# Input tiles with a 64-value slot for each head's 48 values

## The chip, the cores and the metric

The kernel runs on one core of a Trainium2 chip. Its time is the device time of one execution in microseconds (us). Several runs are given by their median. A profile is one execution recorded by the hardware profiler; its span runs from the first to the last recorded instruction.

## What is computed

Two parts follow each other. A gated recurrence runs over 4 batches, 8 heads, 768 steps and a head size of 48, and its output feeds a feed-forward part with the largest of three products in place of an activation.

```python
# q, k, v, alpha: (4, 8, 768, 48) float32
for t in range(S):
    state = alpha[:, :, t, :, None] * state + einsum('bhd,bhe->bhde', k[:, :, t], v[:, :, t])
    y[:, :, t] = einsum('bhd,bhde->bhe', q[:, :, t], state)
# y, heads side by side, becomes x: (3072, 384)
h = maximum(maximum(x @ w1, x @ w2), x @ w3)   # w1, w2, w3: (384, 768)
out = h @ w_out                                # w_out: (768, 384); out: (3072, 384) float32
```

## The kernel before

The recurrence is cut into six blocks of 128 time steps. One step of the kernel takes one block of two batches (16 pairs of batch and head, `NH`), so that there are 12 steps. Time steps stand on the 128 partitions.

For each step, `load` (L81 to L87) fetches four tiles, `ra`, `rk`, `rq` and `rv`, from `alpha`, `k`, `q` and `v`, in this order, by one DMA each on the queue of SyncE (SP, L85). In memory an input is ordered batch, head, time, value; a tile has the time on the partition and 16 x 48 values in it. So one DMA moves 128 x 16 rows of 48 values, which are 192 bytes each, and 384 KB in all. Every one of the four names has four buffers (`raw`, `bufs=4`).

The pieces that read these tiles are few. `logs` (L137) is one ScalarE instruction that takes the logarithm of `ra` into `la`, whose rows are 64 values apart. `decays` multiplies the logarithms by a triangular matrix on TensorE, takes two exponentials on ScalarE, and multiplies `rk` and `rq` by them into `qk` (L159 and L160); this is done on VectorE in steps 0 to 2 and on GpSimd later. `values` (L170) scales `rv` into float16 on ScalarE.

The other pieces work on what these leave. `turn` transposes `qk`, `scores` and `attend` form the outputs of the recurrence, `turn_back` transposes them for the feed-forward part, `gates` (L233 and L235, GpSimd) and `update` (L254, VectorE) carry the state to the next block, `gate` (L268 to L278) forms the three products and their maximum, and `project` (L285 to L290) forms the result and stores it.

The order on every engine is written out by hand in five strings, `PROLOGUE`, `FIRST`, `SECOND`, `STEADY` and `LAST`. A letter is a piece, the digit is a part of it, and `@` gives the step. In the order of SP's queue, the loads of steps 0, 1 and 2 come first (12 DMAs), then 12 DMAs with the weights (L120 and L125), then the loads of steps 3 and 4. From then on `load(s + 3)` stands ahead of each step's pieces, and the stores of the results lie between the loads. GpSimd casts the weights to float16 in groups of three (`cast_weights`, L130, the pieces `W0` to `W3`). In GpSimd's order `W0` stands directly ahead of the gate product of step 0 (`M0@0`).

The tiles are laid out in each partition one after another: first the constant tiles and the weights, then the 16 input tiles of `raw`, then the working tiles.

Of the kernel before, what the change touches and what calls it, by code (L numbers as in the profile page):

```python
# [9 lines left out]
FP32 = mybir.dt.float32  # L10
# [13 lines left out]
def kernel(  # L24
# [14 lines left out]
    B, H, S, D = q.shape  # L39
    NT, DM = out.shape  # L40
    DF = moe_w_out.shape[0]
    P = 128
# [4 lines left out]
    NH = U * H  # L47
# [20 lines left out]
    raw = ctx.enter_context(tc.tile_pool(name="raw", bufs=4))  # L68
# [9 lines left out]
    def where(s):  # L78
        return s // (B // U), (s % (B // U)) * U

    def load(s):  # L81
        cb, b0 = where(s)
        for n in ("a", "k", "q", "v"):
            t = raw.tile([P, NH, D], FP32, name=f"r{n}", tag=f"r{n}")
            nc.sync.dma_start(  # L85
                t, ins[n][cb * P:(cb + 1) * P, b0:b0 + U].rearrange("s b h d -> s (b h) d"))
            raws[s, n] = t  # L87

    c16 = cpool.tile([P, 3 * P + 2], FP16, name="c16")
    c32 = cpool.tile([P, 6], FP32, name="c32")  # L90
    load(0)
    nc.scalar.dma_start(c16, nc.inline_tensor(c16_np, name="c16").ap())
    nc.scalar.dma_start(c32, nc.inline_tensor(c32_np, name="c32").ap())
# [240 lines left out]
    LAST = """G0 G1 G2 G3 G4 G5 G6 G7 O1 G8 O0"""  # L334

    load(1)
    load(2)
    load_weights()
    load(3)
# [43 lines left out]
```

## Time and profile before

| | |
|---|---|
| time, median of two runs | 171.71 us (170.89 and 172.54) |
| span of the profiled execution | 168.8 us |
| TensorE busy | 156.9 us, 93% of the span |
| VectorE busy | 112.2 us, 66% |
| ScalarE busy | 99.0 us, 59% |
| GpSimd busy | 49.0 us, 29% |
| DMA | 107,251 packets, 28.68 MB, of them 99,808 packets under 512 bytes |
| one input load | 384 KB, median from issue to landing 4.7 us (`ra`) to 5.8 us (`rq`) |

For the profiled execution the profile gives the span alone, so its own time outside the span is not known; the median of the two runs lies 2.9 us above the span.

How to read the profile: PE is TensorE's matrix multiplication, PEld its loading of weights, DVE VectorE, ACT ScalarE, POOL GpSimd, SP SyncE. A letter q behind a name is that engine's queue of instructions that issue DMAs or wait. L85 is line 85 of the kernel. In the rows of the slices, the span is cut into 40 equal parts and each digit is the busy share in tenths; PEclk is the clock granted to TensorE in tenths of full speed. The row DMA is the mean share of 16 DMA engines, GB/s what they moved. In a list of waits the columns are who waited, for whom, the sum in us, the number of waits, and the longest. In an order of time they are the start, the duration, the engine, the line, the operation, and in brackets the idle time before it with what ended it. The chain is the work that ended last, followed back step by step to what released it.

### The profile page before, as it was taken

The numbers are of one execution on the slowest core, as the hardware profiler recorded it, in microseconds if no ns is written. First come the engines' busy times: TensorE is split into PE (matmuls) and PEld (weight loads), VectorE is DVE, ScalarE is ACT, GpSimd is POOL, SyncE is SP. The second block draws the span as 40 slices with busy tenths as digits, with TensorE's granted clock in tenths as the row PEclk, the third lists the DMA queues.
The fourth block names the chain that finished last, engine by engine and source line by source line (L and its number), as shares of the span: only waits on it lengthen the run. The fifth ranks groups of instructions, "written<-read, shape, count | busy, mean of one in ns | idle before, by whom it ended". The sixth has DMA issues, their size and how long they took to land.

```text
span 168.8 us, 4329 instructions
## 1 busy us (share of the span) xinstructions
PE 156.9 (93%) x1758; PEld 121.1 (72%) x1758; DVE 112.2 (66%) x185; ACT 99.0 (59%) x181; POOL 49.0 (29%) x72
## 2 busy tenths in 40 slices
PE   7955859999999999999999999999999999999992
PEld 2423637699887676886877978968968869869860
DVE  4186777756647757597587587687667775975730
ACT  3616585142777684874974964956856748435232
POOL 0000005756063454404512531541442244100000
PEclk9995675599999999999999999999999999999999
DMA  6999999998999999999897967948931011020013
GB/s 131 223 219 218 176 247 336 355 360 170 226 172 213 218 248 254 192 226 221 219 223 189 235 105 177 228 91 192 212 92 50 0 56 41 0 93 4 0 47 140
DMA packets 107251, 28.68 MB, mean 170 GB/s; under 512 B 99808, under 2 KB 107232, under 8 KB 107232
## 3 DMA queue, kind: packets, MB, share of 16 engines
q1 hardware_dynamic: 106944, 28.32, 77.3%
q8 instruction: 13, 0.21, 0.6%
q10 hardware_dynamic: 288, 0.10, 0.3%
q14 instruction: 6, 0.05, 0.1%
HBM read 23.69 MB, written 4.72 MB: 168 GB/s over the span
## 4 chain that ended last, share of the span: by engine, by line
PE 81%; SPq 7%; DMA 3%; ACT 3%; DVE 2%; issue 1%; ACTq 0%
PE ops L285 14%; SPq L85 7%; PE tps L179 6%; DMA ra<-in_alpha_dram 3%; PE yps L210 3%; PE xtp L222 2%; PE lps L146 2%; PE yps L207 2%; PE sps L250 2%; PE sps L247 2%; DVE lat L196 1%; PE lps L149 1%; ACT xb L214 1%; PE gps_514 L268 1%; PE gps_523 L268 1%
## 5 line engine op out<-in xcount | busy, mean ns | idle before, releaser
L268 PEld LDWEIGHTS <-wcat 128*128 128x128 f16 x648 | 60.3, 98 | 9.0 <-POOL gm L235 0.2
L285 PE MATMUL ops<-wo_97,hT 128*128 128x384 f16 x144 | 27.1, 327 | 0.0
L288 ACT COPY ob<-ops 128x384 f32<-128x384 f32 x24 | 11.5, 480 | 14.2 <-PE ops L285 14.2
L155 ACT ACTIVATE ic<-lps,c_69 128x384 f32<-128x384 f32 x24 | 13.9, 581 | 8.4 <-PE lps L146 5.1
L285 PEld LDWEIGHTS <-hT 128*128 128x128 f16 x144 | 12.8, 98 | 7.5
L183 DVE COPY qkT<-tps 128x1024 f16<-128x1024 f16 x24 | 16.4, 683 | 1.3 <-PE tps L179 1.1
L214 ACT ACTIVATE xb<-yps,c_69 128x384 f16<-128x384 f32 x24 | 14.0, 585 | 4.8 <-PE yps L210 4.8
L156 ACT ACTIVATE ac<-lps,c_69 128x384 f32<-128x384 f32 x24 | 13.8, 575 | 0.0
L210 PE MATMUL yps<-vt,lat 128*128 128x48 f16 x192 | 12.2, 190 | 0.6 <-ACT vt L170 0.6
L193 PEld LDWEIGHTS <-qkT 48*128 48x128 f16 x192 | 6.3, 98 | 8.8 <-issue 7.7
L159 POOL TENSOR_TENSOR qk_87<-rk,ic 128x384 f16<-128x384 f32 x6 | 6.0, 997 | 21.9 <-ACT ic L155 21.9
L210 PEld LDWEIGHTS <-lat 128*128 128x128 f16 x192 | 10.5, 101 | 1.5 <-DVE lat L196 0.7
L170 ACT ACTIVATE vt<-rv,c_69 128x768 f16<-128x768 f32 x12 | 11.3, 940 | 0.0
L225 ACT COPY xT<-xtp 128x768 f16<-128x768 f16 x12 | 9.6, 803 | 1.0 <-PE xtp L222 1.0
L296 PE MATMUL wps<-blank 128*128 128x512 f16 x22 | 8.0, 528 | 1.2 <-DVE blank L343 1.2
L159 POOL TENSOR_TENSOR qk_86<-rk,ic 128x384 f16<-128x384 f32 x4 | 4.0, 997 | 15.4 <-ACT ic L155 15.4
L130 POOL CAST wcat<-ws_0_114 128x768 f16<-128x768 f32 x1 | 0.8, 823 | 26.3 <-DMA ws_0_114<-in_moe_w_dram 26.3
L159 POOL TENSOR_TENSOR qk_85<-rk,ic 128x384 f16<-128x384 f32 x4 | 4.0, 995 | 13.9 <-ACT ic L155 13.9
L207 PEld LDWEIGHTS <-qkT 128*128 128x128 f16 x80 | 7.7, 98 | 0.4
L222 PE MATMUL xtp<-c_68,xb 128*128 128x128 f16 x72 | 7.4, 228 | 0.5 <-ACT xb L214 0.3
L159 POOL TENSOR_TENSOR qk_84<-rk,ic 128x384 f16<-128x384 f32 x4 | 4.0, 996 | 12.4 <-ACT ic L155 12.4
L222 PEld LDWEIGHTS <-xb 128*128 128x128 f16 x72 | 5.2, 101 | 2.3 <-ACT xb L214 0.9
(409 smaller groups left out, 359.6 us busy)
## 6 DMA issues: line engine op xcount, KB each, us to landing
ra<-in_alpha_dram SPq DMA_DIRECT2D x12, 384.0 KB, 4.7
rk<-in_k_dram SPq DMA_DIRECT2D x12, 384.0 KB, 5.6
rq<-in_q_dram SPq DMA_DIRECT2D x12, 384.0 KB, 5.8
rv<-in_v_dram SPq DMA_DIRECT2D x12, 384.0 KB, 5.7
out_dram<-ob SPq DMA_DIRECT2D x24, 192.0 KB, 2.0
ws_0_114<-in_moe_w_dram SPq DMA_DIRECT2D x1, 384.0 KB, 4.9
ws_1_116<-in_moe_w_dram SPq DMA_DIRECT2D x1, 384.0 KB, 4.5
ws_2_118<-in_moe_w_dram SPq DMA_DIRECT2D x1, 384.0 KB, 5.0
```

Of the source, the lines that this page charges most:

```text
L85: nc.sync.dma_start(t, ins[n][cb * P:(cb + 1) * P, b0:b0 + U].rearrange("s b h d -> s (b h) d"))
L155: nc.scalar.activation(out=ic, in_=lv, func=AFT.Exp, bias=nat_c, scale=-1.0)
L156: nc.scalar.activation(out=ac, in_=lv, func=AFT.Exp, bias=at_c)
L159: eng.tensor_mul(kv, raws[s, "k"][:, hs], ic)
L170: nc.scalar.mul(vt, raws.pop((s, "v")), vs_c)
L183: nc.vector.tensor_copy(out=qkT, in_=tps)
L210: nc.tensor.matmul(yps[:, p, i, :], lat[:, i, p, :], vt[:, u * H + 2 * p + i, :], start=(cb == 0), stop=(cb == 0 or i == 1))
L214: nc.scalar.mul(xb, yps.rearrange("p a b d -> p (a b d)"), ys_c)
L222: nc.tensor.transpose(xtp[:, u, f, :], xb[:, f * P:(f + 1) * P], ident)
L268: nc.tensor.matmul(gps[:, j, :], wcat[:, f, g, jj * P:(jj + 1) * P], xT[:, f].rearrange("p u t -> p (u t)"), start=(f == 0), stop=(f == NF ...
L285: nc.tensor.matmul(ops, hT_of[s][:, jj, u * P:(u + 1) * P], wo16[:, jj, :], start=(jj == 0), stop=(jj == NJ - 1))
L288: nc.scalar.copy(out=ob, in_=ops)
```

## The change

An input tile is declared with 64 places for each pair of batch and head, and the kernel uses the first 48 of each. The values that are loaded, their order and all instructions stay the same; the rows that a load writes are 256 bytes apart instead of 192, and a tile takes 4,096 bytes of each partition instead of 3,072.

```diff
     def load(s):
         cb, b0 = where(s)
         for n in ("a", "k", "q", "v"):
-            t = raw.tile([P, NH, D], FP32, name=f"r{n}", tag=f"r{n}")
+            t = raw.tile([P, NH, 64], FP32, name=f"r{n}", tag=f"r{n}")[:, :, :D]
             nc.sync.dma_start(
                 t, ins[n][cb * P:(cb + 1) * P, b0:b0 + U].rearrange("s b h d -> s (b h) d"))
             raws[s, n] = t
```

## The prediction

> **What bounds the kernel now.** I read the page first (span, slices, chain), then the waits, then the DMA view of the first 15 us, then the order of time of SP's queue and of 26 to 31 us.
>
> ```profile
> span 168.8 us, 4329 instructions
> PE   7955859999999999999999999999999999999992
> DMA  6999999998999999999897967948931011020013
> PEclk9995675599999999999999999999999999999999
> PE 81%; SPq 7%; DMA 3%; ACT 3%; DVE 2%; issue 1%; ACTq 0%
> ```
>
> A slice is 4.2 us. From slice 8 (about 30 us) TensorE is full to the end, so there only TensorE work sets the time. The first seven slices have holes while the DMA row is at 9: this is where loads can decide. The chain agrees: 81% TensorE, and 10% the queue that issues loads and one load.
>
> ```profile
> ACT la_81 L137 <- DMA ra<-in_alpha_dram: 3.5, 1, 3.5
> ACT la_80 L137 <- DMA ra<-in_alpha_dram: 3.5, 2, 3.2
> ACT la_82 L137 <- DMA ra<-in_alpha_dram: 1.7, 1, 1.7
> POOL wcat L130 <- DMA ws_0_114<-in_moe_w_dram: 26.3, 1, 26.3
> ```
>
> All 8.7 us that compute waits for input loads are four waits of ScalarE for an alpha tile, three of them in the first 20 us; GpSimd cannot start casting weights before 26.7 us, when the first weight tile has come through behind twelve input loads.
>
> ```profile
> GB/s 0 0 0 0 6 129 244 277 263 258 236 239 246 230 222 203 224 227 223 211 206 215 232 223 216 218 214 221 219 215 204 228 225 217 212 213 219 224 217 220
> ...
> q1 hardware_dynamic: 14799, 2.82, 112.9%
> ```
>
> This is the DMA view of 0 to 15 us, 0.375 us a slice. With one load under way it moves 244 to 277 GB/s, with a backlog about 220. A load is 2048 rows of 192 bytes, 128 on each of 16 DMA engines; 192 x 16 / 220 = 14.0 ns a row and engine, and 128 x 14.0 = 1.79 us a load. SP's queue has the same step:
>
> ```profile
> 6.45 1.75 SPq L85 DMA_DIRECT2D ra<-in_alpha_dram  x1
> 8.24 1.75 SPq L85 DMA_DIRECT2D rk<-in_k_dram  x1
> 10.04 1.75 SPq L85 DMA_DIRECT2D rq<-in_q_dram  x1
> 11.83 1.75 SPq L85 DMA_DIRECT2D rv<-in_v_dram  x1
> ```
>
> Behind the twelve loads, the start of the feed-forward part hangs on these:
>
> ```profile
> 28.89 0.83 POOL L130 CAST wcat<-ws_2_118 128x768 f16<-128x768 f32 x1 [0.27 <-DMA ws_2_118<-in_moe_w_dram]
> 30.04 0.21 POOL L235 TENSOR_TENSOR gm<-gt,c_69 128x16 f32<-128x16 f32 x1
> 30.28 0.56 DVE L254 TENSOR_TENSOR st_1_89<-sps,gm 128x384 f16<-128x384 f32 x1 [0.34 <-POOL gm L235]
> ```
>
> The third weight tile releases a cast, the cast (same engine) the gate product gm, and gm the state on VectorE, which waited only 0.34 us. So a later load stream passes on nearly one for one, while an earlier one gains only until the other chain (alpha of step 2, landing at 19.4 us, then la_82) is last.
>
> [...] the products at L159 already write strided rows of 48, at 556 ns for 384 values.
>
> **The change, part by part.** The order of instructions on every engine, and SP's waits, stay as they were; only addresses and strides change.
>
> *Where rows come to lie.* The title of the change promises 256-byte boundaries. It gives the pitch, 256 bytes, but not the base. In the built program the first input tile begins 104,384 bytes into each partition, and that is 407 x 256 + 192. Tiles are 3,072 bytes before and 4,096 after, both multiples of 256, so all sixteen begin at 192 beyond a boundary. Before, rows lie at 192, 128, 64, 0 and so on: the first two of four cross a boundary. After, every row lies at 192 and crosses one. So the change doesn't do what it says; if the write side cares for boundaries at all, it is worse off.
>
> *Loads, 48 of 2048 rows.* Bytes, rows and queue order are the same, so HBM's side is. Does the write side set the 14.0 ns? The same tiles, with the same mixture of offsets, were written at 277 GB/s at the start (192 x 16 / 277 = 11.1 ns). So writes in this layout can go at 11.1 ns or better, and what holds a backlog at 14.0 is something else. [...] Lower bound: the opening rate held throughout, 11.1, which is -2.9. I take 0, since the trace has the write side faster than the pace. Each ns costs 12 x 128 x 1 ns = 1.54 us at the first weight tile.
>
> *Engine reads.* 12 logs (L137, 842 ns), 12 value scalings (L170, 948 ns) and 48 products (L159 and L160: 12 on VectorE at 556 ns, 36 on GpSimd at 996 ns) now read rows of 48 with a gap. The logs and products already write such rows. Taken at 0; a bound of +5% would be 24 x 0.045 = 1.1 us on ScalarE, busy 59%, and 36 x 0.05 = 1.8 us on GpSimd, busy 29%, both beside a TensorE that is busy 12.00 of 12 us in the windows from 72 to 120 us. In the prologue, where this cover is missing, it would be three logs, three scalings and 12 products: 3 x 0.042 + 3 x 0.047 + 12 x 0.028 = 0.6 us. For a gain nothing speaks but symmetry; I bound it by the same 0.6.
>
> *Room.* 16 tiles x 1,024 bytes = 16 KB a partition more; the tiles behind move by 16,384 bytes, a multiple of 256, so no other tile changes its offset. 0.
>
> *After the prologue.* A steady step is 11.9 us (from projection at 75.49 us to 87.42), its four loads 4 x 1.79 = 7.2 us: hidden[...].
>
> *The sum.* Span 168.8 + 0 = 168.8. What lies around the span is 171.71 - 168.8 = 2.9 us if the profiled execution was like the median. Predicted 171.7 us.
>
> **Rivals.**
>
> *Slower: each crossing costs on the write side, on top of the 14.0 ns.* Place: L85's twelve loads ahead of the weights. [...] all of it reaches the end, because TensorE is full from there[...]. It decides from 2.2 ns a row (3.4 us, 2%). For it: all rows cross instead of half, the backlog is in this stage, and the step is at SP's heels. Against: 244 to 277 GB/s at the start with half the rows crossing. [...]
>
> *Faster: writes with gaps go quicker for a reason that no view shows* (or the base is aligned after all). At 11.1 ns the ninth load, the alpha of step 2, comes 9 x 128 x 2.9 ns = 3.3 us earlier. la_82 waits 1.7 us itself and its predecessors waited 3.5, so it follows: at best -3.3, 168.4 us, just under 2%; to pass it the pace would have to go below 11.1. For it: these loads are on the chain. Against: the base at 192, the unchanged source side, and that before has the wider mixture including aligned rows.
>
> *Engine reads slow down with the gaps*, the 0.6 us above: 172.3, no change.
>
> **How the numbers follow.** No change 0.60, slower 0.30, faster 0.10. The slower case has much weight because a penalty for crossing can only go one way with this base, and because a load stream that grows later reaches the end undiminished. 2% (3.4 us) is about what a measurement of this kernel can tell from no change; its two runs alone lie 1.65 us apart. The range reaches from the faster case (168.4, rounded into 168.8) to a little over the slower one, 177.5; the likeliest case's own is 170.5 to 173.0.
>
> **What would show it right or wrong.** Right: the load step on SP's queue stays at 1.79 us, the backlog at about 220 GB/s, the first cast at 26.7 us, the first gate at 30.5 us, and L137, L170, L159 keep 842, 948 and 556/996 ns. [...] The faster one shows as a step near 1.5 us, and shorter waits of la_81 and la_82. Durations at L137 or L159 that grow by more than 5% would show the engine reads wrong. A change of the steady step from 11.9 us would make the whole argument wrong, since no part of the change reaches it here.

## The result and the profile after

The changed kernel takes 177.88 us (median of 177.53 and 178.22) against 171.71 us, slower by a ratio of 1.039 (95% interval 1.027 to 1.051). The forecast was no change. The profiled execution took 177.53 us, of which the span is 175.6 us; before it was 168.8 us. For the experiments below, the time is the median of all executions, and the ratio leaves out those in a slower state and compares the rest with the kernel before as measured beside them (medians of all 171.00 us for the first four experiments, 170.77 us for the other four).

The page's span, slices and chain after the change:

```profile
span 175.6 us, 4329 instructions
PE   7844366899999999999999999999999999999992
DMA  7999999999999999999999999999999901010013
PEclk9995576558999999999999999999999999999999
PE 79%; SPq 9%; DMA 4%; ACT 3%; DVE 2%; issue 1%; ACTq 0%
```

The work is the same, and TensorE's busy time nearly so (158.2 us, before 156.9). A slice is now 4.4 us, and TensorE is full from the ninth slice on, at about 35 us instead of 30 us: the holes at the start became longer and the rest kept its length. The two waits for loads ahead of it grew:

```profile
ACT la L137 <- DMA ra<-in_alpha_dram: 17.5, 4, 6.2
POOL wcat L130 <- DMA ws<-in_moe_w_dram: 35.1, 7, 33.1
```

ScalarE's waits for alpha tiles doubled from 8.7 to 17.5 us, and the first weight tile holds GpSimd until 33.6 us instead of 26.7 us. The DMA view of 0 to 15 us, in slices of 0.375 us, shows why:

```profile
GB/s 0 0 0 0 31 200 227 250 249 195 149 159 163 163 163 163 162 163 163 163 164 164 163 163 164 163 163 164 164 162 162 163 164 164 163 163 162 163 165 163
...
q1 hardware_dynamic: 11327, 2.16, 124.0%
```

In the opening the loads run at up to 250 GB/s (before, up to 277). Then, in the backlog, where loads are issued faster than they finish, they sit at 163 GB/s, almost without scatter, where before they had about 220. That is 192 x 16 / 163 = 18.8 ns a row and engine instead of 14.0. SP's queue shows the same step, from start to start:

```profile
7.76 2.35 SPq L85 DMA_DIRECT2D ra<-in_alpha_dram  x1
10.15 2.35 SPq L85 DMA_DIRECT2D rk<-in_k_dram  x1
12.55 2.36 SPq L85 DMA_DIRECT2D rq<-in_q_dram  x1
14.95 2.35 SPq L85 DMA_DIRECT2D rv<-in_v_dram  x1
```

2.40 us a load instead of 1.79. Over twelve loads this is 12 x 0.61 = 7.3 us at the first weight tile. In the order of time on GpSimd and on VectorE:

```profile
33.58 0.82 POOL L130 CAST wcat<-ws 128x768 f16<-128x768 f32 x1 [33.14 <-DMA ws<-in_moe_w_dram]
...
36.04 0.83 POOL L130 CAST wcat<-ws 128x768 f16<-128x768 f32 x1 [0.57 <-DMA ws<-in_moe_w_dram]
...
37.20 0.21 POOL L235 TENSOR_TENSOR gm<-gt,c 128x16 f32<-128x16 f32 x1
...
37.44 1.02 DVE L254 TENSOR_TENSOR st<-sps,gm 128x384 f16<-128x384 f32 x2 [1.42 <-POOL gm L235]
```

The first cast starts 6.85 us later (26.73 before), the gate product 7.16 us (30.04), the state 7.16 us (30.28), and the span is 6.8 us longer. But these pieces are not what the end waited for. The chain runs over another load, the alpha of step 2, the ninth. First before, then after:

```profile
13.63 5.76 DMA ra<-in_alpha_dram
...
30.58 1.39 PE gps_514 L268 x6
```

```profile
17.34 7.67 DMA ra<-in_alpha_dram
...
36.66 2.67 PE gps L268 x12
```

That load lands 5.6 us later (25.0 us for 19.4), and the first gate on TensorE starts 6.1 us later (36.59 us for 30.51), 2.2 us after its weights have been cast. The 36 gate matmuls that follow the next outputs of the recurrence take 4.5 us (39.80 to 44.31) instead of 3.9 (33.72 to 37.66), at a lower granted clock: it was 0.75 from 40 to 42 us, and before 1.00 from 34 to 36 us. These two make 6.7 of the 6.8 us. All other steps stand still: L137 has a median of 844 ns, L170 948 ns, L159 556 ns on VectorE and 1,002 ns on GpSimd, and a steady step takes 11.94 us (projection at 82.23 and 94.17 us in the chain).

### The profile page after: what moved, and what is told of

It reads as the page before. It is cut to its first block, busy times and chain, and to the rows that moved or that the text cites. A ratio compares the mean times of both kernels' runs of the same rounds, so it can differ in the third digit from the quotient of the medians.

```text
span 175.6 us, 4329 instructions
## 1 busy us (share of the span) xinstructions
PE 158.2 (90%) x1758; PEld 121.9 (69%) x1758; DVE 112.3 (64%) x185; ACT 99.1 (56%) x181; POOL 49.3 (28%) x72
## 4 chain that ended last, share of the span: by engine, by line
PE 79%; SPq 9%; DMA 4%; ACT 3%; DVE 2%; issue 1%; ACTq 0%
PE gps L268 42%; PE ops L285 14%; SPq L85 9%; PE tps L179 6%; PE aps L193 5%; DMA ra<-in_alpha_dram 4%; PE xtp L222 3%; PE yps L210 2%; PE lps L146 2%; PE yps L207 2%; PE sps L250 2%; PE sps L247 1%; DVE lat L196 1%; PE lps L149 1%; ACT ic L155 1%
## 5 line engine op out<-in xcount | busy, mean ns | idle before, releaser
L268 PE MATMUL gps<-xT,wcat 128*128 128x256 f16 x648 | 83.4, 276 | 0.0
L278 DVE TENSOR_TENSOR h<-gps,h 128x512 f16<-128x512 f32 x36 | 24.9, 692 | 22.0 <-PE gps L268 18.5
L276 ACT CAST h<-gps 128x512 f16<-128x512 f32 x36 | 21.1, 587 | 29.2 <-PE gps L268 28.8
L196 DVE TENSOR_TENSOR lat<-aps,c 128x512 f16<-128x512 f32 x48 | 30.8, 684 | 10.2 <-PE aps L193 10.2
L159 POOL TENSOR_TENSOR qk<-rk,ic 128x384 f16<-128x384 f32 x18 | 18.0, 1002 | 61.0 <-ACT ic L155 58.0
L278 DVE TENSOR_TENSOR hT<-gps,h 128x512 f16<-128x512 f32 x36 | 24.9, 692 | 11.1 <-PE gps L268 9.4
L285 PE MATMUL ops<-wo,hT 128*128 128x384 f16 x144 | 27.1, 327 | 0.0
L179 PE MATMUL tps<-c,qk 128*128 128x128 f16 x192 | 15.9, 231 | 6.4 <-DVE qk L160 6.0
L137 ACT ACTIVATE la<-ra 128x768 f16<-128x768 f32 x12 | 10.1, 845 | 17.5 <-DMA ra<-in_alpha_dram 17.5
L288 ACT COPY ob<-ops 128x384 f32<-128x384 f32 x24 | 11.5, 482 | 13.4 <-PE ops L285 13.4
L160 POOL TENSOR_TENSOR qk<-rq,ac 128x384 f16<-128x384 f32 x18 | 18.0, 1000 | 2.4 <-DMA rq<-in_q_dram 2.4
L214 ACT ACTIVATE xb<-yps,c 128x384 f16<-128x384 f32 x24 | 14.1, 586 | 4.9 <-PE yps L210 4.9
```

Of the source, the lines that this page charges most:

```text
L159: eng.tensor_mul(kv, raws[s, "k"][:, hs], ic)
L160: eng.tensor_mul(qv, raws[s, "q"][:, hs], ac)
L179: nc.tensor.transpose(tps[:, i, p, :], qk[:, i, u * HP + p].rearrange("p a b -> p (a b)"), ident)
L196: nc.vector.tensor_mul(lat[:, i], aps[i], mask.unsqueeze(1).broadcast_to([P, HP, P]))
L268: nc.tensor.matmul(gps[:, j, :], wcat[:, f, g, jj * P:(jj + 1) * P], xT[:, f].rearrange("p u t -> p (u t)"), start=(f == 0), stop=(f == NF ...
L276: nc.scalar.copy(out=h, in_=gps)
```

## The experiments

The offset of a row is how far behind a 256-byte boundary of its partition it begins. Three theories were set against each other. A: a row that a load writes is paid by the 256-byte blocks that it touches, so one that crosses a boundary costs twice. B: the price of a row grows with its offset. C: the gap between rows costs, wherever they begin. Before, the pace of 14.0 ns fits A (one and a half blocks of 9.4 ns, half of the 18.8 after) and B (offsets of 96 bytes on average, where after they are 192) alike. A straight line through these two paces, as an estimate, gives B 12.4 ns at offset 64 and 15.6 ns at 128; what tells them apart is the offset.

### Rows at offset 0

The edit is against the changed kernel.

```diff
+    lead = ctx.enter_context(tc.tile_pool(name="lead", bufs=1))
+    lead.tile([P, 16], FP32, name="lead")     # 64 bytes: input tiles begin at 104,448 = 408 x 256
     raw = ctx.enter_context(tc.tile_pool(name="raw", bufs=4))
+    tail = ctx.enter_context(tc.tile_pool(name="tail", bufs=1))
+    tail.tile([P, 48], FP32, name="tail")     # 192 bytes: the tiles behind keep their offset
```

> The changed kernel with 64 bytes put ahead of the input tiles (and 192 behind them), so that every tile begins on a 256-byte boundary and each 192-byte row lies at offset 0 and crosses none. Theory A, a row is paid by the 256-byte blocks that it touches (9.4 ns a block: one block 9.4, two 18.8, before with one and a half on average 14.1): the write side falls below the pace of about 12.5 ns that the opening of the first load shows, so SP's queue steps at about 1.60 us a load, the backlog is near 245 GB/s, the first cast comes near 24.4 us, and the time is about 170.0 us, a little below before. [...] Theory C, the gap between rows itself costs, wherever the base is: as the changed kernel, 2.40 us a load, 163 GB/s, 177.9 us.

170.93 us, ratio to the kernel before 0.996 (0.993 to 0.999). SP's queue, the issues of two alpha loads that are four loads apart:

```profile
6.21 1.74 SPq L89 DMA_DIRECT2D ra<-in_alpha_dram  x1
...
13.09 1.45 SPq L89 DMA_DIRECT2D ra<-in_alpha_dram  x1
```

6.88 / 4 = 1.72 us a load (1.60 was expected), 13.4 ns a row (1.72 us over 128 rows). Sixty-four bytes of padding take the whole loss away; C falls, since the gap is the same. The gain over the kernel before is smaller than the load step promises. First the cast, on GpSimd, then the first gate on TensorE, then the page's shares of the chain:

```profile
25.34 2.00 POOL L134 CAST wcat<-ws 128x768 f16<-128x768 f32 x2 [24.90 <-DMA ws<-in_moe_w_dram]
...
30.18 1.48 PE L272 MATMUL gps<-xT,wcat 128*128 128x256 f16 x12
...
PE 85%; DVE 6%; DMA 3%; ACT 2%; issue 1%; SPq 1%; DVEq 0%; ACTq 0%
```

The cast is 1.39 us earlier than before, the gate only 0.33 us (30.51 before), because the chain has changed: SP's queue has 1% of it instead of 7%. The last load on it ahead of the first gate is the q of step 0, which landed at 7.8 us; from there on the chain is the work of TensorE, VectorE and ScalarE on the first steps, which faster loads don't shorten.

### Rows at offset 64

Here and at offset 128, the edit is shown against that of offset 0; the tail shrinks by what the lead grows.

```diff
-    lead.tile([P, 16], FP32, name="lead")
+    lead.tile([P, 32], FP32, name="lead")     # 128 bytes, and 128 behind
```

> The same with 128 bytes ahead (128 behind): every row at offset 64, from 64 to 256, up to a boundary and not across it. Theory A (blocks): as with offset 0, 1.60 us a load, about 170.0 us. [...] Theory C (gap): 2.40 us a load, 177.9 us.

171.12 us, ratio 0.995 (0.991 to 0.999).

```profile
6.46 1.88 SPq L89 DMA_DIRECT2D ra<-in_alpha_dram  x1
...
13.20 1.60 SPq L89 DMA_DIRECT2D ra<-in_alpha_dram  x1
```

6.74 / 4 = 1.69 us, 13.2 ns, no worse than offset 0 (13.4 ns). For the load's pace, a row may begin inside a block as long as it ends in it: the alignment of the start is not what counts. A and B can't be told apart here: both price such a row (9.4 and 12.4 ns) below what was measured.

### Rows at offset 128

```diff
-    lead.tile([P, 16], FP32, name="lead")
+    lead.tile([P, 48], FP32, name="lead")     # 192 bytes, and 64 behind
```

> The same with 192 bytes ahead (64 behind): every row at offset 128, half of its... that is from 128 to 320, across one boundary. Theory A (blocks): two blocks as in the changed kernel, 18.8 ns, 2.40 us a load, 163 GB/s, 177.9 us. [...] Theory C (gap): 2.40 us, 177.9 us; A and C are told apart by offsets 0 and 64.

177.95 us, ratio 1.043 (1.036 to 1.049).

```profile
7.44 2.35 SPq L89 DMA_DIRECT2D ra<-in_alpha_dram  x1
...
17.01 2.31 SPq L89 DMA_DIRECT2D ra<-in_alpha_dram  x1
```

9.57 / 4 = 2.39 us, 18.7 ns: as at offset 192 (18.8 ns), and not the 15.6 ns of theory B. The split of a row, into 128 and 64 bytes here, 64 and 128 at offset 192, makes no difference. B falls.

### Large tiles, packed rows

The edits from here on are against the changed kernel.

```diff
-            t = raw.tile([P, NH, 64], FP32, name=f"r{n}", tag=f"r{n}")[:, :, :D]
+            t = raw.tile([P, NH * 64], FP32, name=f"r{n}", tag=f"r{n}")
+            t = t[:, :NH * D].rearrange("p (h d) -> p h d", d=D)
```

> Tiles of 4,096 bytes as in the changed kernel, at the same addresses, but the 768 values packed at their front as before, rows 192 bytes apart. Theories A, B and C all expect the kernel before: 1.79 us a load, 220 GB/s, 171.7 us. A rival D, that the larger tiles or the moved working tiles behind them cost the time: as the changed kernel, 177.9 us, with 1.79 us a load.

171.40 us, ratio 0.998 (0.993 to 1.002).

```profile
6.47 1.75 SPq L86 DMA_DIRECT2D ra<-in_alpha_dram  x1
...
13.65 1.72 SPq L86 DMA_DIRECT2D ra<-in_alpha_dram  x1
```

1.795 us a load, as before. The size of the tiles and the shift of those behind cost nothing that the ratio shows; D falls.

### Rows 224 bytes apart

```diff
-            t = raw.tile([P, NH, 64], FP32, name=f"r{n}", tag=f"r{n}")[:, :, :D]
+            t = raw.tile([P, NH, 56], FP32, name=f"r{n}", tag=f"r{n}")[:, :, :D]   # with the 64 bytes ahead
```

> Input tiles that begin on a 256-byte boundary, with 56 places a head: rows 224 bytes apart, at offsets 0, 224, 192, 160, 128, 96, 64 and 32, of which five of eight cross a boundary. If each 256-byte block that a row touches costs 9.4 ns (theory A), a row costs 1.625 x 9.41 = 15.3 ns: 1.96 us a load on SP's queue, about 201 GB/s in the backlog, the first cast near 28.4 us, about 172.9 us. If any gap that isn't a whole 256 bytes, or a start that isn't a multiple of 64 bytes, costs more (rival E), the pace is above that, up to or past the 18.8 ns of the changed kernel.

172.45 us, ratio 1.010 (1.004 to 1.016). SP's queue, and the first cast on GpSimd:

```profile
6.58 1.90 SPq L89 DMA_DIRECT2D ra<-in_alpha_dram  x1
...
14.34 1.88 SPq L89 DMA_DIRECT2D ra<-in_alpha_dram  x1
```

```profile
28.31 0.82 POOL L134 CAST wcat<-ws 128x768 f16<-128x768 f32 x1 [27.87 <-DMA ws<-in_moe_w_dram]
```

7.76 / 4 = 1.94 us, 15.2 ns, where A gave 15.3 before the run; the cast came at 28.3 us for an expected 28.4. Rows that begin at 32, 96, 160 and 224, no multiples of 64, add nothing of their own. E falls. The kernels together:

| rows at offsets (of 256) | blocks a row | load step, us | ns a row | blocks x 9.4 ns |
|---|---|---|---|---|
| 0 | 1 | 1.72 | 13.4 | 9.4 |
| 64 | 1 | 1.69 | 13.2 | 9.4 |
| 192, 128, 64, 0 (before) | 1.5 | 1.79 | 14.0 | 14.1 |
| 0, 224, 192 ... 32 | 1.625 | 1.94 | 15.2 | 15.3 |
| 128 | 2 | 2.39 | 18.7 | 18.8 |
| 192 (after) | 2 | 2.40 | 18.8 | 18.8 |

With one block a row the load goes at 13.2 to 13.4 ns, above the 9.4 of the block, so something else sets the pace there. What that is wasn't settled. It doesn't hold row by row: if each row of one block took 13.3 ns and each of two 18.8, the kernel before would go at 16.1, and it goes at 14.0. Blocks of another size, priced the same way, don't fit. Of 128-byte blocks, a row touches two at each of the offsets 0, 64, 128 and 192, whose paces differ by over 5 ns. Of 512-byte blocks, a row touches 1.25 before and 1.5 after, a ratio of 1.20 where the paces stand as 1.34.

### The first twelve loads alone, and the others alone

First, the changed kernel with packed rows in steps 0 to 2:

```diff
-            t = raw.tile([P, NH, 64], FP32, name=f"r{n}", tag=f"r{n}")[:, :, :D]
+            t = raw.tile([P, NH * 64], FP32, name=f"r{n}", tag=f"r{n}")
+            w = D if s < 3 else 64
+            t = t[:, :NH * w].rearrange("p (h d) -> p h d", d=w)[:, :, :D]
```

> The changed kernel, but the twelve loads of steps 0 to 2 are packed as before; the loads of steps 3 to 11 keep the 64-value slots at offset 192, where every row crosses. If only the loads ahead of the weights pass their delay on to the end: the kernel before, 171.0 us, at most 0.5 us more, though the later loads run at 18.8 ns a row. If the later loads matter too (rival F: they make steps 3 and 4 late, or compete with the stores), part of the 7 us comes back: 173 us or more.

171.77 us, ratio 1.008 (1.005 to 1.011). The first cast and the waits for alpha tiles:

```profile
27.07 0.82 POOL L132 CAST wcat<-ws 128x768 f16<-128x768 f32 x1 [26.63 <-DMA ws<-in_moe_w_dram]
```

```profile
ACT la L139 <- DMA ra<-in_alpha_dram: 11.1, 5, 3.6
```

Then the mirror (`w = 64 if s < 3 else D`):

> The mirror: the loads of steps 0 to 2 have the slots of the changed kernel, where every row crosses, and the loads of steps 3 to 11 are packed as before. If the first twelve loads make the whole difference: the changed kernel, 177.9 us, at most 0.5 us less. Under rival F, clearly less, 176 us or below.

177.39 us, ratio 1.040 (1.033 to 1.046), with the first cast as late as in the changed kernel:

```profile
33.68 0.82 POOL L132 CAST wcat<-ws 128x768 f16<-128x768 f32 x1 [33.24 <-DMA ws<-in_moe_w_dram]
```

The first twelve loads make the whole loss; that of these only the nine on the chain matter was not tried by itself. The later ones are not free: alone they cost 0.8%, 1.3 us by the ratio (1.0 us by the medians), more than the 0.5 us expected, and the list shows a fifth wait for an alpha tile and 2.4 us more in all. TensorE's busy time in the window from 60 to 72 us, before and with packed first loads (columns: length, busy time and count of PE, PEld, DVE, ACT and POOL, granted clock, DMA share, GB/s):

```profile
60.00:72.00 12.00, 11.93 (x149) 9.59 (x150) 8.03 (x14) 8.79 (x18) 5.50 (x10) 1.00 1.04 231
```

```profile
60.00:72.00 12.00, 11.37 (x142) 8.96 (x143) 7.87 (x13) 8.18 (x16) 4.85 (x7) 1.00 1.11 200
```

The alpha of step 4 comes close to when it is needed: it was waited for 0.27 us before and is for 2.29 us here, and that of step 5 for 0.67 us. With packed first loads both lie on the chain (DMA has 13% of it, before 3%); in the changed kernel and in the mirror neither does. The two losses don't add: the mirror alone has all of the 3.9%. That the later start of the compute in it leaves the later loads more room fits, but was not tried by itself.

### Weights on a boundary as well

```diff
-    c32 = cpool.tile([P, 6], FP32, name="c32")
+    c32 = cpool.tile([P, 24], FP32, name="c32")[:, :6]   # all tiles behind move by 64 bytes
```

> 64-value slots with all tiles moved up by 64 bytes (a wider constant tile ahead of them), so that the input tiles and the weights' float32 tiles begin on a 256-byte boundary. Theory A: the input loads go as with aligned input tiles alone, 13.1 ns a row; a 1,024-byte weight row touches four blocks instead of five, so its price falls from 5 x 9.41 = 47 ns (350 GB/s, as before shows) to 37.6 ns or what another limit sets, above 380 GB/s, and the nine weight loads take about 1 us less. The time is that of the aligned input tiles, 170.3 us, or up to 1 us below. If weight rows don't follow the price by block: 350 GB/s, and 170.3 us.

171.04 us, ratio 1.001 (0.998 to 1.004). The GB/s of weight loads, before from 28 to 36 us and here from 27 to 35 us:

```profile
GB/s 236 271 241 338 369 394 358 369 374 384 364 343 379 348 358 358 343 369 353 353 353 343 338 353 353 348 348 343 358 343 343 356 348 348 356 443 335 353 361 369
```

```profile
GB/s 343 210 236 256 276 333 369 389 389 389 364 394 384 374 394 379 374 384 384 399 364 399 384 364 410 379 369 399 379 394 376 397 389 463 379 376 356 384 387 387
```

Behind the first six slices, the median is 384 GB/s instead of 353: 1,024 x 16 / 353 = 46.4 ns for five blocks (5 x 9.4 = 47.0) and 42.7 ns for four, above the 37.6 of four blocks, so something else holds them. At five blocks the price holds for rows of another size; at four it was not seen. In the time nothing of it is seen, and the chain shows why: as at offset 0, the last load on it before the first gate is the q of step 0 (landed at 8.1 us), and no weight load is among its pieces. The expected microsecond took the weights to be there. Why the time is not as low as at offset 0 isn't known.

No version beats the kernel before by an amount that counts: offsets 0 and 64 gain 0.4% and 0.5% by the ratio, with intervals that end just below no change, and nothing by the medians of all executions (170.93 and 171.12 us against 171.00).

## Why the prediction was wrong

*What bounds the kernel* was right in the main: the input loads at the start are on the chain, their delay reaches the end, and the steady step stayed at 11.9 us. The route was misread. It was put down to the third weight tile, the gate product and the state, but in the kernel before the state was ready at 30.84 us and TensorE first read it at 33.04:

```profile
33.04 0.29 PE L207 MATMUL yps<-st_1_89,qkT 128*128 128x96 f16 x1
```

The chain ran over the alpha of step 2, nine loads and not twelve. The prediction used that route for its faster rival alone.

*Where rows come to lie* was right, and it is the reason for the loss. The change gives the pitch, not the base; at 192 every row crosses a boundary where half did. With the base moved by 64 bytes the same edit costs nothing (170.93 us, ratio 0.996).

*Engine reads, room, order* were right at nothing: the durations at L137 (844 ns), L170 (948 ns) and L159 (556 and 1,002 ns) stand within 1%, and large tiles with packed rows run as before (1.795 us a load, ratio 0.998).

*Loads* is the step that failed: the term was taken at 0, and each row took 4.8 ns more. It argued that the same layout had been written at 277 GB/s in the opening, so the write side could do 11.1 ns a row and was not what held a backlog at 14.0. The profile after shows that the opening is no measure of what the write side sustains: with every row crossing, it still has up to 250 GB/s for about 1.5 us, and then 163. It is about one load long (the six slices from 31 to 195 GB/s moved 0.43 MB, a load is 0.39 MB), but not a state with one load under way, as the prediction called it: SP's queue issued the second load from 1.22 to 2.64 us in the kernel before. Why it is faster stays open. That the sustained 220 GB/s was the write side, at one and a half blocks a row, is what the offsets show: the pace follows the blocks at 1.5, 1.625 and 2, and falls a little at one.

*The price* was the second error. The price that the slower rival put on a crossing, and that served as the upper bound, was the author's estimate; no trace or run showed it. Measured were +4.8 ns (18.8 - 14.0), more than it allowed, since a second block is charged in full, whatever part of it is written (18.7 ns with 64 bytes in it, 18.8 with 128). So the slower rival had the mechanism and the stage, and even its upper bound was not an upper bound. That the end of the range, 177.5 us, comes so near to 177.88 is partly luck: too low a price was taken over twelve loads, where 4.8 ns over the nine on the chain make 5.5 us. The rival was passed over on the strength of the opening rate alone.

## What to carry to other kernels

Padding the pitch aligns nothing unless the base is aligned too (2.40 us a load with the base at 192, 1.72 at 0): work out the address of the first row in the built layout before counting on it. Count the 256-byte blocks that each written row touches: for the 192-byte rows here that count, and not the bytes, set the load's pace from one and a half blocks on (14.0 ns a row at 1.5, 15.2 at 1.625, 18.8 at 2). Before pricing a delay, follow the chain to the load that is on it: a short wait further down, as of the state for gm, need not be what the end waits for. Take a sustained rate from the middle of a long backlog, never from the first microsecond of it (up to 277 GB/s against about 220 before, 250 against 163 after).

## What the runs showed of the hardware

A row of a load cost 9.4 ns for each 256-byte block of the partition that it touched, at 1.5, 1.625 and 2 blocks (14.0, 15.2 and 18.7 to 18.8 ns); with a single block it took 13.2 to 13.4 ns, and why was not shown. How a row is divided between its two blocks made no difference (18.7 ns at offset 128, 18.8 at 192), nor did a start inside a block that is not crossed (13.2 ns at offset 64, 13.4 at 0). In about the first 1.5 us of the loads after the change, rates up to 250 GB/s stood ahead of a sustained 163 GB/s. Why a block has this price was not shown.
